# Linear attention and two MLPs on one core: the first eight steps of h written out in a set order

## The chip, the cores and the metric

One core of a Trainium2 chip runs the whole program. Its engines are named as the profile names them: PE (TensorE, matmuls; PEld its weight loads), DVE (VectorE), ACT (ScalarE), POOL (GpSimd) and SP (SyncE, which here issues loads and stores). The time is device microseconds of one execution, the median over several runs. Lower is better.

## The reference

```python
kv  = einsum('bhsd,bhse->bhde', k, v)          # batch 8, heads 8, seq 576, head_dim 64
out = einsum('bhsd,bhde->bhse', q, kv)
x   = out / sqrt(mean(out * out, -1) + 1e-6) * g_norm     # -> 4608 tokens x 512
h   = x @ w_in                                 # 512 -> 2048
x   = (h * cos(h)) @ w_out                     # 2048 -> 512
x   = ((x @ w1) * (x @ w2) @ w3) @ w_out2      # 512 -> 1024 -> 1024 -> 512
```

All values are float32.

## The kernel before

A token block is 512 tokens (nine blocks), a unit is half a batch, 288 tokens (16 units). Heads go in four pairs of 128 rows. The first MLP runs in steps n: in each, `emit_h` makes 128 columns of h (m) for a block (12 matmuls of 512 columns, since a float32 factor is split into a high and a low half and three products are summed), `g_first` and `g_rest` make g = h cos h of it on ACT and DVE, split into halves, and `emit_w(n-2)` adds g of two steps back to x (12 matmuls into four PSUM banks `acc0` to `acc3`). The order of the steps is m = 0 to 7 of block 0, then all 16 of block 1, then m = 8 to 15 of block 0, then the rest. Here x in the profile is the result of `emit_w`, and the operand of h too, by its tile.

The parts of g in a step: r = rounding of h / 2 pi (ACT), u = h / 2 pi - r (DVE), Sin (ACT), u times h (DVE), high half (ACT), low half (DVE).

The weights come in 32 blocks of 64-bit words in an order set by `first_pairs` (`i` for w_in, `u` for w_out: i0, i1, i2, u0, i3, u1, i4, u2, ...). `Chunk.convert` turns one block into float32: an absolute value on ACT (L141), then four passes on DVE (L142, L143, L146, L149). `put` splits the result into halves (ACT L112, DVE L114). The float rows of a block, u and others share five `row` buffers. Loads are issued by `prefetch`.

`load_first` issues the loads of the first two batches (k and v per pair `kvraw`, the last 64 rows of all pairs `kvrest` in one tile with one buffer, q per pair) between those of the first weight blocks, all on SP but two q loads. `first_batch` makes units 0 and 1: kv, out by a 128 x 128 matrix (`whole`, two heads on its diagonal), squares, sums of squares per token by matmuls, norms by a Newton iteration on DVE (`norms`), then `emit_rows`: the norms spread over partitions by 12 small matmuls for each unit and pair (`spread`), and one DVE product (L507). `split_x` makes the halves of x, the operand of h.

`second_batch` does the same for units 2 and 3 during steps 0 to 5 of the main loop. Its pieces are hung into steps by a plan with five places in a step: kv of pair p and unit 2 in step p, unit 3 one step later, the norms in step 5, and all rows of the spread behind them. Each out goes to one of two PSUM banks of `ps_a`, through the pool. All conversions of blocks from step 6 on are issued behind the norms (`second_last`). Block 1's x needs these units, so step 8 of h does too.

What sets the order: inside `tc.manual_schedule` PE, ACT and DVE take their instructions in the order of the program; before, that covers `first_batch` alone. All other work, SP's loads at all times too, is put in order by the scheduler of the framework, by readiness in its own model of time and by the order of the program; `tc.issue_after` adds an edge. On the chip each engine and SP's queue then take their instructions in that fixed order.

Of the kernel before, what the change touches and what calls it, by code (L numbers as in the profile page):

```python
# [1 line left out]

# [31 lines left out]
def kernel(  # L34
# [59 lines left out]
    def stage(shape, dtype, name):  # L94
        return ap.tile(shape, dtype, tag="stage", bufs=2, name=name)
# [311 lines left out]
    def load_first():  # L407

        def kv(b, p, q):
            t = wpool.tile(  # L410
                [P, 2, NC, P], F32, tag=f"wi{NM - 2 * NPAIR + p}", name=f"kvraw_{b}_{p}"
            )
            q.dma_start(
                out=t.rearrange("p i c f -> p (i c f)"),
                in_=kv_main[b, p].rearrange("p i c f -> p (i c f)"),
            )
            kv_raw[b, p] = t

        def rest(b, q):
            t = ap.tile([P, NPAIR // 2, 2, P], F32, tag="rest", name=f"kvrest_{b}")  # L420
            q.dma_start(
                out=t.rearrange("p g i f -> p (g i f)"),
                in_=kv_tail[b].rearrange("p g i f -> p (g i f)"),
            )
            kv_rest[b] = t

        def qs(b, p, q):
            t = wpool.tile([P, 2, HALF], F32, tag=f"wi{NM - NPAIR + p}", name=f"q_{b}_{p}")
            q_raw[b, p] = t
            q.dma_start(out=t, in_=qt[b, p].rearrange("u d s -> d u s"))  # L430

        qs(0, 0, nc.scalar)
        qs(0, 1, nc.scalar)
        for h in range(2):
            nc.scalar.dma_start(
                out=gneg[D * h:D * h + D], in_=g_norm.rearrange("(d o) -> d o", o=1)
            )
        kv(0, 0, nc.sync)
        rest(0, nc.sync)
        kv(0, 1, nc.sync)  # L440
        prefetch(1)
        kv(0, 2, nc.sync)
        qs(0, 2, nc.sync)
        prefetch(2)
        kv(0, 3, nc.sync)
        qs(0, 3, nc.sync)
        prefetch(7)
        for p in range(NPAIR):
            if p == NPAIR - 1:
                rest(1, nc.sync)  # L450
                prefetch(8)
            kv(1, p, nc.sync)
            qs(1, p, nc.sync)

    whole = []
# [4 lines left out]
            d = slice(D * h, D * (h + 1))  # L460
            nc.scalar.activation(whole[p][d, d], ps[d], AF.Copy)

    def emit_whole(u, p, pl, tag):
        ps = pl.tile([P, 512], F32, tag=tag, name=f"out_{u}_{p}")[:, 0:HALF]
        q = q_raw[u // NHALF, p][:, u % NHALF]
        nc.tensor.matmul(ps, whole[p], q, start=True, stop=True)
        o_ps[u, p] = ps

    squares = {}
    second_last = []  # L470

    def column(u, k, p):
        return ((u % NHALF * NT3 + k) * NPAIR + p) * 2
# [20 lines left out]
        nc.vector.tensor_scalar(x, sums[0:T3, 0:NR], EPS, HUGE, ALU.add, ALU.min)  # L494
        return newton(x, y, t)

    def emit_rows(u, p, ps, y, spread):
        for k in range(NT3):
            at = column(u, k, p)
            for h in range(2):  # L500
                mm = nc.tensor.matmul(
                    ps[D * h:D * h + D, T3 * k:T3 * k + T3],
                    y[:, at + h:at + h + 1].to_broadcast([T3, D]), spread,
                    start=k == 0, stop=True, skip_group_check=True,
                )
        o = o_sb[u][:, p, :]
        nc.vector.tensor_tensor(o, o, ps[:, 0:HALF], ALU.mult)  # L507
        return mm.ins

    def first_batch(spread, x, y, t):  # L510
# [19 lines left out]
        made = None  # L530
        for p in range(NPAIR):
            for u in units:
                emit_whole(u, p, ps_acc, f"acc{(2 * p + u) % 4}")
            for u in units:
                emit_square(u, p)
            if p == 0:
                made = pieces(count[0])
            rest_of(made)
            if p > 0:
                put(count[p - 1])  # L540
            if p + 1 < NPAIR:
                emit_kv(0, p + 1)
                copy_kv(p + 1)
            if p == 0:
                nc.vector.tensor_scalar(gneg, gneg, -1.0, None, ALU.mult)
            for u in units:
                emit_sums(u, p, sums, fresh=True)
            for u in units:
                emit_keep(u, p)
            if p + 1 < NPAIR:  # L550
                made = pieces(count[p + 1])
        norms(sums, x, y, t)
        put(count[-1])
        for p in range(NPAIR + 1):
            if p < NPAIR:
                for u in units:
                    ps = ps_acc.tile(
                        [P, 512], F32, tag=f"acc{(2 * p + u) % 4}", name=f"spread_{u}_{p}"
                    )
                    mm = emit_rows(u, p, ps, y, spread)  # L560
            if p > 0:
                last = split_x(0, p - 1)
        return mm, last

    def second_batch(spread, x, y, t):

        units = range(NHALF, 2 * NHALF)
        banks = {}

        def kv(p):  # L570
            if p == 0:
                banks[0] = ps_a.tile([P, 512], F32, tag="pa", name="kv_second")
            emit_kv(1, p, banks[0])

        def evac(u, p):
            emit_square(u, p)
            emit_keep(u, p)

        def sums(u, p):
            emit_sums(u, p, banks[0][:, NPAIR * D:NPAIR * D + NR])  # L580

        def rows(u, p):
            ps = ps_a.tile([P, 512], F32, tag="pa", name=f"spread_{u}_{p}")
            emit_rows(u, p, ps, y, spread)

        def last_norms():
            second_last.append(norms(banks.pop(0)[:, NPAIR * D:NPAIR * D + NR], x, y, t))

        plan = {}

        def at(n, i, f, *a):
            plan.setdefault(n, ([], [], [], [], []))[i].append(lambda: f(*a))

        a, b = units
        for p in range(NPAIR):
            at(p + 1, 0, emit_whole, b, p, ps_a, "pa")
            at(p + 1, 1, evac, b, p)
            at(p + 1, 3, sums, b, p)
        for p in range(NPAIR):
            at(p, 0, kv, p)  # L600
            at(p, 1, copy_kv, p)
            at(p, 2, emit_whole, a, p, ps_a, "pa")
            at(p, 2, evac, a, p)
            at(p, 3, sums, a, p)
        at(NPAIR + 1, 4, last_norms)
        for p in range(NPAIR):
            at(NPAIR + 1, 2 + p // 2, rows, a, p)
            at(NPAIR + 1, 2 + p // 2, rows, b, p)
        return plan

    NEWTON, LAST = 8, 10

# [44 lines left out]
    x0_d = dram.tile([P, KD, TB], F32, name="x0")  # L657
    part0_d = dram.tile([P, KD, TB], F32, name="part0")
    halfway = {}

    def save_x0():
        for u in range(2):
# [62 lines left out]
    def emit_w(n):  # L725
        t, m, first, last = steps[n]
        g = g_hl.pop(n)
        for j in range(KD):
            if first:
                acc[j] = ps_acc.tile([P, 512], F32, tag=f"acc{j}", name=f"x2_{n}_{j}")  # L730
            w = w_out[m][:, :, j * P:(j + 1) * P]
            three(acc[j], (w[:, 0], w[:, 1]), (g[:, 0], g[:, 1]), first, last)
        if last:
            for j in range(KD):
                s = row(f"x2s_{n}_{j}")
# [5 lines left out]
                    nc.vector.tensor_copy(s, acc[j])  # L741
                dst = part0_d[:, j] if m < NM - 1 else x2_d[:, j, t * TB:(t + 1) * TB]
                nc.sync.dma_start(out=dst, in_=s)

# [278 lines left out]
    if True:  # L1025
# [25 lines left out]
        with tc.manual_schedule(  # L1051
            engines={
                mybir.EngineType.DVE, mybir.EngineType.Activation, mybir.EngineType.PE
            }
        ):
            tiles = [spread] + [firsts[0:T3, T3 + NR * i:T3 + NR * i + NR] for i in range(3)]
            spread_last, split_last = first_batch(*tiles)
        behind = ExitStack()
        behind.enter_context(tc.issue_after(spread_last))
        for ins in split_last:  # L1060
            behind.enter_context(tc.issue_after(ins))
        second = second_batch(*tiles)

        NS = NB * NM
        ready = 4
# [6 lines left out]
            for u, s in zip(new, starts):  # L1072
                windows[u] = t * NM + s

        save_x0()
        since = []
        for n in range(NS + 2):
            t, m, first, last = steps[n] if n < NS else (NB, n - NS, False, False)
            swap = first and 0 < n
            if swap:  # L1080
                emit_w(n - 2)
            stages = []
            if n == NM + HM:
                load["alone"] = False
            ahead = 2 * n + 6 if n < 7 else 18 + (n - 7) * 6 // 5
            more = min(n_first, ahead) - state["conv"] if n < NS else 0
            if n < NS:
                with tc.issue_after(word_loads[min(n + 9, n_first - 6, len(word_loads) - 1)].ins):
                    stages = [
                        unit_stage(u, n - w) for u, w in windows.items() if 0 <= n - w <= LAST  # L1090
                    ]
                if n in second:
                    stages += [second[n]]
                    for f in second[n][4]:
                        f()
                if more > 0:
                    prefetch(min(state["conv"] + 8, n_first))
                    with tc.issue_after(second_last[0]) if second_last else nullcontext():
                        convert(more)
                emit_h(n)  # L1100
                uu = g_first(n)
            gate = ExitStack()
# [24 lines left out]
            with ExitStack() as gate:  # L1127
# [1 line left out]
                    for ins in since[:24][-3:] if n > 8 else ():  # L1129
                        gate.enter_context(tc.issue_after(ins))  # L1130
                run(stages, 3)
            if n == 7:
                behind.close()
            if n == NM + 4:
                load_halves("x0", x0_d)
            if n == 2 * NM - 4:
# [191 lines left out]
```

## Time and profile before

| | before |
|---|---|
| median of 3 runs | 1528.65 us (1527.91 to 1529.38) |
| profiled execution, own time | 1531.0 us |
| span of its trace | 1528.9 us |
| PE busy | 1491.9 us, 98% |
| DVE, ACT, POOL busy | 865.7, 674.6, 350.0 us |
| mean granted clock of PE | 0.985 |

The span runs from the first instruction to the last. Busy PE says that a matmul was in flight, not that PE ran at its peak; the granted clock is 1.00 at 2.4 GHz and 0.50 at 1.2 GHz. Of the page's 40 slices (38.2 us each) PE is below nine tenths in the first (six tenths) and the third (seven tenths), and the granted clock falls to seven tenths in the same two.

### The profile page before, as it was taken

The page shows a single profiled execution, that of the slowest core. Times are in us where ns is not written, and L with a number is a line of the kernel's source. Part 1 is how long each engine was busy: PE and PEld are TensorE (multiplying, and loading weights), DVE is VectorE, ACT ScalarE, POOL GpSimd, SP SyncE. Part 2 cuts the span into 40 slices and gives each one's busy share as a digit, 9 for nine tenths or more (in the row PEclk, how much of TensorE's full clock was granted, in tenths as well). Part 3 has the DMA queues.
Part 4 walks back from the last instruction along what each step waited for, and adds up shares of the span by engine and source line. Part 5 has one row for each costly group of instructions (what it writes and reads, how often), then busy time and mean ns, then how long its engine had stood idle before and what let it go on. Part 6 is the DMA issues. An engine that isn't in the chain of part 4 may idle for free.

```text
span 1528.9 us, 20580 instructions
## 1 busy us (share of the span) xinstructions
PE 1491.9 (98%) x7728; PEld 1275.0 (83%) x7728; DVE 865.7 (57%) x1559; ACT 674.6 (44%) x1355; POOL 350.0 (23%) x278
## 2 busy tenths in 40 slices
PE   6979999999999999999999998999999999999998
PEld 5757878878887887888888886999999988999997
DVE  5867845466565555555555337755545546545543
ACT  4635554544454454454535335443433334333331
POOL 0000010110010111101102006455444237344330
PEclk7979999999999999999999999999999999999999
DMA  9414330533423435334223015121112313233312
GB/s 361 155 43 147 102 91 17 157 106 106 126 86 109 140 105 150 89 109 130 89 73 101 10 41 193 42 76 67 67 40 83 110 57 104 82 104 125 124 62 76
DMA packets 81299, 155.02 MB, mean 101 GB/s; under 512 B 11232, under 2 KB 36944, under 8 KB 81200
## 3 DMA queue, kind: packets, MB, share of 16 engines
q1 hardware_dynamic: 80224, 152.08, 30.8%
q8 instruction: 60, 0.98, 0.3%
q0 software_dynamic: 272, 1.05, 0.2%
q10 hardware_dynamic: 704, 0.59, 0.1%
q14 instruction: 39, 0.32, 0.1%
HBM read 112.57 MB, written 41.12 MB: 101 GB/s over the span
## 4 chain that ended last, share of the span: by engine, by line
PE 93%; DVE 3%; DMA 1%; POOL 1%; issue 1%; SPq 0%; ACT 0%; DVEq 0%; ACTq 0%
PE X L928 13%; PE h L696 9%; PE x L696 9%; PE h L697 9%; PE h L698 9%; PE x L697 9%; PE x L698 9%; PE V L928 6%; PE o L697 4%; PE o L696 4%; PE o L698 4%; PE Y L928 3%; PE kv L277 1%; DMA i_w<-in_w1pair_dram 1%; DMA u_w<-in_w1pair_dram 1%
## 5 line engine op out<-in xcount | busy, mean ns | idle before, releaser
L928 PE MATMUL X<-xc,w 128*128 128x384 f32 x1152 | 226.3, 337 | 4.5 <-DVE wchl L114 2.3
L697 PE MATMUL x<-g,w_out 128*128 128x512 f32 x576 | 225.3, 391 | 0.0
L715 DVE SCALAR_TENSOR_TENSOR u<-h,r 128x512 f32<-128x512 f32 x144 | 99.5, 691 | 221.9 <-ACT r L713 218.3
L698 PE MATMUL x<-g,w_out 128*128 128x512 f32 x576 | 224.4, 390 | 0.0
L696 PE MATMUL x<-g,w_out 128*128 128x512 f32 x576 | 219.0, 392 | 0.0
L696 PE MATMUL h<-x,w_in 128*128 128x512 f32 x544 | 215.4, 396 | 3.0 <-DVE u L720 3.0
L928 PEld LDWEIGHTS X<-xc,w 128*128 128x128 f32 x1152 | 204.4, 189 | 12.0 <-ACT s L936 3.2
L697 PE MATMUL h<-x,w_in 128*128 128x512 f32 x544 | 214.1, 394 | 0.0
L698 PE MATMUL h<-x,w_in 128*128 128x512 f32 x544 | 213.2, 392 | 0.0
L114 POOL TENSOR_TENSOR xc<-x2r,xc 128x768 fp32r<-128x768 f32 x70 | 134.7, 1934 | 228.8 <-ACT xc L112 224.4
L713 ACT ACTIVATE r<-h 128x512 int32<-128x512 f32 x144 | 86.0, 597 | 220.6 <-PE h L698 210.8
L114 POOL TENSOR_TENSOR qhl<-q,qhl 128x288 fp32r<-128x288 f32 x48 | 41.1, 857 | 464.2 <-ACT qhl L112 464.2
L112 ACT ACTIVATE g<-u 128x512 fp32r<-128x512 f32 x144 | 90.9, 631 | 109.5 <-DVE u L720 83.0
L114 DVE TENSOR_TENSOR g<-u,g 128x512 fp32r<-128x512 f32 x144 | 104.4, 725 | 60.8 <-ACT g L112 60.7
L936 ACT ACTIVATE s<-X 128x384 f32<-128x384 f32 x144 | 66.6, 488 | 152.4 <-PE X L928 152.3
L696 PEld LDWEIGHTS x<-g,w_out 128*128 128x128 f32 x576 | 108.1, 188 | 22.9
L720 DVE TENSOR_TENSOR u<-u,h 128x512 f32<-128x512 f32 x144 | 98.6, 685 | 50.5 <-ACT u L719 50.3
L696 PEld LDWEIGHTS h<-x,w_in 128*128 128x128 f32 x544 | 103.0, 189 | 28.8 <-DVE u L720 7.0
L698 PEld LDWEIGHTS x<-g,w_out 128*128 128x128 f32 x576 | 108.2, 188 | 22.3
L697 PEld LDWEIGHTS x<-g,w_out 128*128 128x128 f32 x576 | 108.1, 188 | 22.2
L698 PEld LDWEIGHTS h<-x,w_in 128*128 128x128 f32 x544 | 102.8, 189 | 21.3
L697 PEld LDWEIGHTS h<-x,w_in 128*128 128x128 f32 x544 | 102.8, 189 | 20.2
(177 smaller groups left out, 2471.6 us busy)
## 6 DMA issues: line engine op xcount, KB each, us to landing
x2r<-x_all SPq DMA_DIRECT2D x44, 384.0 KB
kvraw<-in_kv_main_dram SPq DMA_DIRECT2D x32, 512.0 KB
x_all<-x2s SPq DMA_DIRECT2D x36, 256.0 KB
part<-o SPq DMA_DIRECT2D x36, 256.0 KB
part<-part SPq DMA_DIRECT2D x36, 256.0 KB
out_dram<-part SPq DMA_DIRECT2D x36, 256.0 KB
i_w<-in_w1pair_dram SPq DMA_DIRECT2D x16, 512.0 KB
u_w<-in_w1pair_dram SPq DMA_DIRECT2D x16, 512.0 KB
```

What stands on the lines that cost most here:

```text
L112: hi = nc.scalar.activation(dst[:, 0], src, AF.Copy)
L114: lo = lo_engine.tensor_tensor(dst[:, 1], src, f32(dst[:, 0]), ALU.subtract)
L277: nc.tensor.matmul(ps[d], k[:, d], v[:, d], start=fresh and i == 0, stop=i == NC, skip_group_check=True,)
L696: nc.tensor.matmul(ps, w[0], x[0], start=first, stop=False)
L697: nc.tensor.matmul(ps, w[0], x[1], start=False, stop=False)
L698: return nc.tensor.matmul(ps, w[1], x[0], start=False, stop=last).ins
L713: nc.scalar.activation(r, h_ps[n], AF.Identity, bias=0.25, scale=INV_2PI)
L715: nc.vector.scalar_tensor_tensor(u, h_ps[n], INV_2PI, r, ALU.mult, ALU.subtract)
L720: nc.vector.tensor_tensor(u, u, h_ps.pop(n), ALU.mult)
L928: nc.tensor.matmul(ps, w[:, self.i, a, k], x[:, b, k], start=first and k == 0 and n == 0, stop=last and k == 1 and n == 2, skip_group_chec ...
L936: copied.append(nc.scalar.activation(s, ps, AF.Copy).ins)
```

## The change

Steps 0 to 7 leave the main loop. A new function `first_steps` writes them out under `manual_schedule`, so PE, ACT and DVE take them in the order of the program. kv of pairs 0 and 1 of batch 1 is made in `first_batch`, ahead of the first norms; kv of pairs 2 and 3 in step 1. From step 2 on units 2 and 3 of one pair go together: each unit has one PSUM bank for its out of all pairs, and the sums of squares lie in the bank of unit 2. Two weight blocks are taken up in each of steps 0 to 5 (and two at the start), and converted in the next step, their DVE passes standing between the parts of g. The norms stand at the end of step 5, the spreads in steps 6 and 7, the split of x for block 1 in step 7. The rounding r goes to a `stage` buffer. The loads are put in another order in the program, and gneg's sign is turned on ACT. The main loop starts at step 8 with one block a step.

```diff
 load_first:
         qs(0, 3, nc.sync)
-        prefetch(7)
+        prefetch(6)
+        rest(1, nc.sync)
+        kv(1, 0, nc.sync)
+        kv(1, 1, nc.sync)
+        prefetch(8)
         for p in range(NPAIR):
-            if p == NPAIR - 1:
-                rest(1, nc.sync)
-                prefetch(8)
-            kv(1, p, nc.sync)
+            if p >= 2:
+                kv(1, p, nc.sync)
             qs(1, p, nc.sync)
 first_batch:
-                nc.vector.tensor_scalar(gneg, gneg, -1.0, None, ALU.mult)
+                nc.scalar.activation(gneg, gneg, AF.Copy, scale=-1.0)
...
+        for p in range(2):
+            emit_kv(1, p)
         norms(sums, x, y, t)
         put(count[-1])
+        for p in range(2):
+            copy_kv(p)
-    def second_batch(spread, x, y, t):
...
+    def first_steps(spread, x, y, t):
...
+        def begin():
+            st = chunks[state["conv"]].convert()
+            state["conv"] += 1
+            next(st)
+            return st
+        def each():
+            for st in pair:
+                next(st)
+        def out_bank(v, p):
+            if p == 0:
+                banks[v] = ps_a.tile([P, 512], F32, tag="pa", name=f"out_{v}")
+            emit_whole(v, p, banks[v][:, 0:HALF])
+        def rows(p):
+            for v in units:
+                spread_ps[v, p] = ps_a.tile([P, 512], F32, tag="pa", name=f"spread_{v}_{p}")
+                emit_rows(v, p, spread_ps[v, p], y, spread, False)
+        def scale(p):
+            for v in units:
+                o = o_sb[v][:, p, :]
+                ps = spread_ps.pop((v, p))
+                nc.vector.tensor_tensor(o, o, ps[:, 0:HALF], ALU.mult)
+        prefetch(min(state["put"] + 8, n_first))
+        pair = [begin(), begin()]
+        for n in range(HM):
+            p = n - 2
+            last = n == HM - 1
+            emit_h(n)
+            if n == 1:
+                for k in (2, 3):
+                    emit_kv(1, k)
+                    copy_kv(k)
+                for v in units:
+                    out_bank(v, 0)
+            if 0 <= p < NPAIR:
+                for v in units:
+                    emit_square(v, p)
+                sums = banks[units[0]][:, HALF:HALF + NR]
+                for v in units:
+                    emit_sums(v, p, sums)
+            if n == NPAIR + 2:
+                rows(0)
+            if n >= 2:
+                emit_w(n - 2)
+            if n == 0:
+                for _ in range(3):
+                    each()
+            if last:
+                scale(1)
+                rows(2)
+            r = stage([P, TB], I32, f"r_{n}")
+            u = row(f"u_{n}")
+            nc.scalar.activation(r, h_ps[n], AF.Identity, bias=0.25, scale=INV_2PI)
+            nc.vector.scalar_tensor_tensor(u, h_ps[n], INV_2PI, r, ALU.mult, ALU.subtract)
+            if n > 0:
+                each()
+                each()
+            nc.scalar.activation(u, u, AF.Sin, bias=HALF_PI, scale=TWO_PI)
+            if last:
+                for c in range(2):
+                    split_x(1, c)
+            new = [begin()] if n < HM - 2 else []
+            nc.vector.tensor_tensor(u, u, h_ps.pop(n), ALU.mult)
+            if n > 0:
+                each()
+            if last:
+                scale(2)
+                rows(3)
+            g_hl[n] = m1.tile([P, 2, TB], F32R, tag="g", bufs=2, name=f"g_{n}")
+            since.extend([h_last.pop(n), *split(g_hl[n], u, nc.vector)])
+            new += [begin()] if n < HM - 2 else []
+            if 0 <= p < NPAIR:
+                for v in units:
+                    emit_keep(v, p)
+            if 1 < n <= NPAIR:
+                for v in units:
+                    out_bank(v, n - 1)
+            if n == NPAIR + 2:
+                scale(0)
+                rows(1)
+            each()
+            put(len(pair))
+            pair = new
+            prefetch(min(state["put"] + 8, n_first))
+            if n == NPAIR + 1:
+                norms(sums, x, y, t)
+        split_x(1, 2)
+        scale(3)
+        made = split_x(1, 3)
+        return [emit_w(HM - 2), *made]
 the main loop:
-        for n in range(NS + 2):
+        for n in range(HM, NS + 2):
...
-            ahead = 2 * n + 6 if n < 7 else 18 + (n - 7) * 6 // 5
+            ahead = 12 + n
...
-                    with tc.issue_after(second_last[0]) if second_last else nullcontext():
-                        convert(more)
+                    convert(more)
```

Here NPAIR is 4 and HM is 8.

## Rows read from the trace of the kernel before

**Rows 1.** The page, chain of waits by engine.

```profile
PE 93%; DVE 3%; DMA 1%; POOL 1%; issue 1%; SPq 0%; ACT 0%; DVEq 0%; ACTq 0%
```

**Rows 2.** Windows: stretch, length, busy per engine (instructions), granted clock, DMA, GB/s.

```profile
41.00:91.80 50.80, 50.24 (x302) 40.26 (x300) 32.13 (x63) 30.38 (x67) 0.26 (x1) 1.00 0.31 104
...
114.00:116.80 2.80, 2.80 (x8) 2.22 (x7) 1.81 (x3) 0.63 (x1) 0.00 (x0) 0.50 0.00 0
116.80:120.00 3.20, 3.20 (x15) 2.65 (x15) 0.00 (x0) 0.00 (x0) 0.00 (x0) 1.00 0.00 0
```

**Rows 3.** Timeline of PE: start, us, instruction; in brackets the idle before it.

```profile
94.56 1.21 PE L501 MATMUL spread<-rs_first 96*64 96x96 f32 x24 [2.75 <-DVE rs_first L370]
96.85 2.26 PE L501 MATMUL spread<-rs_first 96*64 96x96 f32 x24 [1.07 <-DVE o L507]
...
111.22 0.79 PE L696 MATMUL h<-x,w_in 128*128 128x512 f32 x1 [2.83 <-DVE u L720]
...
116.87 0.39 PE L696 MATMUL h<-x,w_in 128*128 128x512 f32 x1
```

**Rows 4.** Timeline of DVE: the first operation of the norms, the first behind them.

```profile
91.86 0.20 DVE L494 TENSOR_SCALAR rs_first<-kv_second 96x48 f32<-96x48 f32 x1 [2.02 <-PE kv_second L488]
...
94.34 0.42 DVE L142 TENSOR_SCALAR i_f<-i_f 128x512 f32<-128x512 f32 x1
```

**Rows 5.** Groups of PE, 38 to 112 us: busy us, mean ns.

```profile
L698 PE MATMUL x<-g,w_out 128*128 128x512 f32 x24 | 9.5, 394 | 0.0
```

**Rows 6.** Timeline of PE in the first batch.

```profile
19.46 0.48 PE L277 MATMUL kv<-kvrest 64*64 64x64 f32 x4
...
31.82 7.29 PE L501 MATMUL spread<-rs_first 96*64 96x96 f32 x96 [5.38 <-DVE rs_first L370]
```

**Rows 7.** Timeline of SP's queue: when each load is issued.

```profile
10.85 0.44 SPq L132 DMA_DIRECT2D u_w<-in_w1pair_dram  x1
...
19.50 0.33 SPq L132 DMA_DIRECT2D i_w<-in_w1pair_dram  x1
...
24.36 0.33 SPq L132 DMA_DIRECT2D u_w<-in_w1pair_dram  x1
...
27.70 0.33 SPq L421 DMA_DIRECT2D kvrest<-in_kv_tail_dram  x1
...
33.73 0.33 SPq L132 DMA_DIRECT2D u_w<-in_w1pair_dram  x1
```

**Rows 8.** The chain in order of time: start, us, what.

```profile
10.85 8.57 DMA u_w<-in_w1pair_dram
```

**Rows 9.** Timeline of DVE: last splits of the first batch, then neighbours of each kind.

```profile
39.65 1.42 DVE L114 TENSOR_TENSOR x<-o,x 128x288 fp32r<-128x288 f32 x4
...
97.05 0.41 DVE L143 TENSOR_SCALAR u_f<-u_f 128x512 int32<-128x512 int32 x1
97.39 0.44 DVE L507 TENSOR_TENSOR o<-o,spread 128x288 f32<-128x288 f32 x1
97.75 0.67 DVE L146 SCALAR_TENSOR_TENSOR i_f<-i_w,i_f 128x512 int32<-128x512 int32 x1
98.35 0.67 DVE L146 SCALAR_TENSOR_TENSOR u_f<-u_w,u_f 128x512 int32<-128x512 int32 x1
```

**Rows 10.** Timeline of ACT: two copies of kv; square, keep, block, Sin in a row.

```profile
44.20 0.43 ACT L461 ACTIVATE rs_first<-kv_second 64x64 f32<-64x64 f32 x2
...
70.02 0.41 ACT L479 ACTIVATE sq<-out 128x288 f32<-128x288 f32 x1 [1.75 <-PE out L466]
70.32 0.50 ACT L482 ACTIVATE o<-out,gneg 128x288 f32<-128x288 f32 x1
70.70 0.67 ACT L141 ACTIVATE i_f<-i_w 128x512 f32<-128x512 f32 x1
71.28 0.61 ACT L719 ACTIVATE u<-u 128x512 f32<-128x512 f32 x1
```

**Rows 11.** Timeline of PE: out of one unit and pair.

```profile
74.70 0.73 PE L466 MATMUL out<-q,rs_first 128*128 128x288 f32 x2
```

More of the change, by code (lines that the diff above doesn't have):

```diff
@@ L1 @@
-from contextlib import ExitStack, nullcontext
+from contextlib import ExitStack
 import concourse.bass as bass
@@ L461, in copy_kv, with emit_whole @@
             nc.scalar.activation(whole[p][d, d], ps[d], AF.Copy)
-    def emit_whole(u, p, pl, tag):
-        ps = pl.tile([P, 512], F32, tag=tag, name=f"out_{u}_{p}")[:, 0:HALF]
+    def emit_whole(u, p, ps):
         q = q_raw[u // NHALF, p][:, u % NHALF]
@@ L469 @@
     squares = {}
-    second_last = []
     def column(u, k, p):
@@ L495, in norms, with emit_rows @@
         return newton(x, y, t)
-    def emit_rows(u, p, ps, y, spread):
+    def emit_rows(u, p, ps, y, spread, scaled=True):
         for k in range(NT3):
@@ L505, in emit_rows @@
                 )
-        o = o_sb[u][:, p, :]
-        nc.vector.tensor_tensor(o, o, ps[:, 0:HALF], ALU.mult)
+        if scaled:
+            o = o_sb[u][:, p, :]
+            nc.vector.tensor_tensor(o, o, ps[:, 0:HALF], ALU.mult)
         return mm.ins
@@ L532, in first_batch @@
             for u in units:
-                emit_whole(u, p, ps_acc, f"acc{(2 * p + u) % 4}")
+                emit_whole(u, p, ps_acc.tile(
+                    [P, 512], F32, tag=f"acc{(2 * p + u) % 4}", name=f"out_{u}_{p}"
+                )[:, 0:HALF])
             for u in units:
@@ L561, in first_batch @@
             if p > 0:
-                last = split_x(0, p - 1)
-        return mm, last
-    def second_batch(spread, x, y, t):
+                split_x(0, p - 1)
+    def first_steps(spread, x, y, t):
         units = range(NHALF, 2 * NHALF)
-        banks = {}
-        def kv(p):
-            if p == 0:
[L572 to L609, printed above, removed]
@@ new lines, in first_steps @@
+        banks, spread_ps = {}, {}
+        def begin():
[7 more added lines that the diff above has]
+        def out_bank(v, p):
+            if p == 0:
+                banks[v] = ps_a.tile([P, 512], F32, tag="pa", name=f"out_{v}")
[4 more added lines that the diff above has]
+                emit_rows(v, p, spread_ps[v, p], y, spread, False)
@@ new lines, in scale @@
+        def scale(p):
+            for v in units:
+                o = o_sb[v][:, p, :]
+                ps = spread_ps.pop((v, p))
+                nc.vector.tensor_tensor(o, o, ps[:, 0:HALF], ALU.mult)
+        prefetch(min(state["put"] + 8, n_first))
[62 more added lines that the diff above has]
+                norms(sums, x, y, t)
@@ L659 @@
     halfway = {}
+    since = []
     def save_x0():
@@ L731, in emit_w @@
             w = w_out[m][:, :, j * P:(j + 1) * P]
-            three(acc[j], (w[:, 0], w[:, 1]), (g[:, 0], g[:, 1]), first, last)
+            mm = three(acc[j], (w[:, 0], w[:, 1]), (g[:, 0], g[:, 1]), first, last)
         if last:
@@ L743, in emit_w @@
                 nc.sync.dma_start(out=dst, in_=s)
+        return mm
     PAIR = {1: (0, 0), 2: (1, 1), 3: (6, 2), 4: (2, 6), 5: (3, 3), 6: (4, 4), 7: (5, 5)}
@@ L1056 @@
             tiles = [spread] + [firsts[0:T3, T3 + NR * i:T3 + NR * i + NR] for i in range(3)]
[L1057 to L1062, printed above, removed]
+            first_batch(*tiles)
+            save_x0()
+            behind = first_steps(*tiles)
         NS = NB * NM
@@ L1073 @@
                 windows[u] = t * NM + s
-        save_x0()
-        since = []
-        for n in range(NS + 2):
+        gates = ExitStack()
+        for ins in behind:
+            gates.enter_context(tc.issue_after(ins))
+        for n in range(HM, NS + 2):
             t, m, first, last = steps[n] if n < NS else (NB, n - NS, False, False)
             swap = first and 0 < n
-            if swap:
+            if swap and n > HM:
                 emit_w(n - 2)
@@ L1091 @@
                     ]
[L1092 to L1095, printed above, removed]
                 if more > 0:
                     prefetch(min(state["conv"] + 8, n_first))
-                    with tc.issue_after(second_last[0]) if second_last else nullcontext():
-                        convert(more)
+                    convert(more)
                 emit_h(n)
@@ L1131 @@
                 run(stages, 3)
-            if n == 7:
-                behind.close()
+            if n == HM + 1:
+                gates.close()
             if n == NM + 4:
```

## The prediction

> **What bounds the kernel now.** I read the chain of waits first. 93% of it is TensorE (PE) [rows 1], so a change pays only where PE stands idle or runs at the lower of its two clock levels (1.2 GHz, shown as 0.50; the higher, 2.4 GHz, as 1.00). The windows come second: from 41.0 to 91.8 us PE is dense at 1.00, then comes a hole, and from 116.8 on it is dense at 1.00 again; a step of h and a step of x, 12 matmuls each, flow at 3.20 us / 14 = 0.23 us a matmul there, 2.76 us a step [rows 2]. The hole lies around the norms of units 2 and 3: PE waits 2.75 us for the last Newton operation of VectorE (DVE), the clock falls, and step 8 of h starts at 111.22 after another wait of 2.83 us and stays at 0.50 until 116.8 [rows 2, 3]. The norms take from 91.86 to 94.34, 2.48 us [rows 4]. In the hole PE does nothing but 96 tiny spread matmuls. Step 8 of h stands behind steps 0 to 7, and 72 matmuls of x are issued by then (three lines of 24, so steps 0 to 5) [rows 5]; at 116.87 step 8 and one matmul of step 9 are through as well. From there nothing in front of PE is late. So I work out when the changed kernel reaches the same amount of PE work; that difference is the answer.
>
> **The change, part by part.** Sums are made against the profiled execution: span 1528.9, own time 1531.0, which is 2.35 above the median 1528.65. A difference in the span is put on both.
>
> *The first batch.* kv of pairs 0 and 1 of batch 1 moves ahead of the first norms, into a stretch where PE waits: after the sums it idles until the spread starts at 31.82 [rows 6]. 40 small matmuls by themselves cost nothing there. But PE takes its instructions in order, and each kv ends with four matmuls on the rest tile (kvrest). That tile has one buffer, so its second load can't be issued before kv(0,3) has read the first, which ends at 19.46+0.48=19.9 [rows 6]. In what order SP issues is set by the scheduler, for SP isn't among the three engines in set order: i5 of a much later step left at 19.50, ahead of rest(1), which left at 27.70 although rest(1) stands earlier in the program [rows 7]. SP also runs eight loads ahead and no more: u_w, issued at 10.85, landed 8.57 later at 19.42 [rows 8], and the eighth issue behind it left at 19.50; so u3, issued 24.36, landed at 33.73, when the eighth behind it left [rows 7]. Between u_w and u3 lie nine loads of 512 KB and two of 288 KB (q), 5184 KB in 33.73-19.42=14.3 us: 1.4 us for 512 KB, 0.8 for a q, 0.7 for the rest tile's 256 KB. Behind u3 come q(1,2), kv(1,3) and rest(1), so rest(1) lands at 33.73+0.8+1.4+0.7=36.6 in its present place, at 35.2 if it goes ahead of kv(1,3). In the new program text it stands further up, but its readiness, kv(0,3), is the same; I take 35.2. Then PE still has the rest of kv(1,0), 0.4, and kv(1,1), about 1.5 at the lower clock (20 matmuls, of which the last four take 0.48 [rows 6], the other 16 about 1.0): the spread starts at 37.1 instead of 31.8, **5.3 us late**. All of this was under no cover but the wait for the norms, which ends at 31.8. The ends: 0 (the load lands before 29.9) and 6.7. The negation of gneg moves from DVE to ScalarE (ACT) and shortens ACT's wait for it, but the first batch then waits for u_w at 19.42 [rows 8] as before: 0.
>
> *Step 0.* After the last split of the first batch DVE is free at 39.65+1.42=41.07 [rows 9] (all times now without the 5.3). It first runs three passes over two blocks, 2x0.34+2x0.34+2x0.6=2.54, so its first operation on h stands at 43.6. The spacings are 0.34 for a TENSOR_SCALAR, 0.60 for the others of 512 columns, 0.36 for a scale, and a 512-column result is there 0.67 after its start [rows 9]. Step 0 has no passes between its parts of g: 0.67, Sin 0.6, 0.67, hi 0.62, lo 0.6, two passes 1.2, then the puts; before r of step 1 ACT still has both hi halves and the four copies of kv(1,2) and kv(1,3), two of which took 0.43 [rows 10]. That is 6.7 us.
>
> *Steps 1 to 5.* DVE has per step 3x0.6 for g, 3.76 for two blocks, 1.2 for their lo halves: 6.8. Were that all, a step would last 7.45 (behind the last hi half, at 6.3, come two squares of 0.3 and r, 0.6 [rows 10]); so step 1. In steps 2 to 4 a loop through three engines is longer. From the start of DVE's first operation: u and four passes 1.96, product ready 2.63, hi 3.27, one block's Abs 0.58 to 3.85, two keeps 0.38 each and their end, 4.7 [rows 9, 10]. Only then may the out bank be overwritten: the out of two units, two matmuls each that last 0.73 with their end [rows 11], so about 1.3 together, and behind these in PE's order the next h: 2.76, its result 0.3 later (a matmul lasts 0.39, and the next one starts after 0.23 [rows 2, 5]), r 0.6: **9.65 us a step**, of which PE idles about 2. Three such steps are 29. Step 5 has no out bank but the norms at its end: 6.95+2.48=9.4 [rows 4].
>
> *Steps 6, 7.* PE has run out of work when h of step 6 is through, some 3.9 us before the norms end. In the kernel before, a wait of 2.75 and one of 1.07 a little later made the clock fall: the same 24 spread matmuls took 1.21 ahead of the second wait and 2.26 behind it [rows 3], so I take the lower clock here, until 5.6 us after PE resumes (111.22 to 116.8). The spread of pair 0 (24 matmuls) 2.3, x of step 4 until 6.7, the spread of pair 1 1.2, h of step 7 2.76 + 0.3, r 0.6: 11.6. At full clock it would be 9.9. In step 7 u, Sin, two column blocks of the x split, the product, two scales and the spread of pair 3 stand in one line until 5.75; x of step 6 and h of step 8 follow at 2.76 each: 11.3.
>
> *The sum.* 43.6+6.7+7.45+29+9.4+11.6+11.3=119.05 for the end of step 8 of h, with x of step 6 done. Before, PE stood 11 matmuls further back at 116.87: 116.87+11x0.23=119.4. So the set order by itself gains 0.35. Against it stand 5.3 for the rest tile, and 0.9 for the clock in step 2: PE waits from 46.5 to 49.8 for the copies of kv and from 53.3 to 57.3 for the squares of pair 0, both longer than the 2.75 of [rows 3], so the sums and x of step 0 start at the lower clock (13 matmuls in 116.87-111.22: 0.43 each), which lasts 5.6 us as there, and end at 63.4, 0.9 behind the keeps at 62.5. 0.35-5.3-0.9 = -5.85. For steps 3 and 4 I take no fall of the clock, bounds 0 and 4.8 (2.4 more for each h at 0.43). Behind step 8 both kernels are dense: 0. Against the profiled execution 1531.0+5.85=1536.85; against the median **1534.5 us**.
>
> One rule of the Trainium skill weighs against the change: "TensorE: Matmul & The Clock Gate", section on PSUM-queue depth-cycling, tells of a kernel in which short idle times between matmul groups, as PSUM banks go round, make the clock swing. This trace shows a fall after waits of 2.75 and 1.07 us [rows 3], and no wait of 2 us between dense groups. By the rule the later steps would swing too and the sum be that of the first rival, 1538.1; by the row, as I read it, 1534.5.
>
> **Rivals.**
> *The clock falls in every step.* For it: the same waits come back each 9.65 us. Against it: a step at the lower clock leaves PE no idle time, so it climbs again. Three h steps at 0.43 cost 3x2.4=7.2, half of that if every other one climbs: 1534.5+3.6=1538.1, at most 1541.7.
> *The rest tile is in time* (not slower). Place: SP's queue. If the scheduler puts rest(1) so far up that SP stands still for it from 13.5 until 19.9, it lands some 4 us later, and kv is hidden. Decides: a landing before 29.9 costs nothing and leaves -0.55, and at 32.4 the loss passes 0.2%. For it: the program text has rest(1) ahead of kv(1,0). Against it: [rows 7]. 1534.5-5.3=1529.2; if the clock also holds in step 6 (1.7), 1527.5, faster by a little.
> *The loop through keep, out and h doesn't bind*, as where out is issued ahead of its place or ACT gets to the keeps sooner: 3x(9.65-7.45)=6.6 less: 1527.9, and 1522.6 with the rest tile in time, which is faster. Against it: three engines in set order.
>
> **How the numbers follow.** The forecast holds 0.40 (its own range 1531.5 to 1537.5), the clock 0.14, the rest tile in time 0.23, the loop 0.17, anything else 0.06. 0.2% is 3.06 us, about what a measurement can tell: under 1525.6 faster, over 1531.7 slower. Slower: 0.35 of the forecast, 0.13 of the clock, 0.03 of the rest tile, 0.01 of the loop = 0.52. Faster: 0.07 of the rest tile, 0.10 of the loop where both go well, 0.03 of the others = 0.20. Same: 0.28. The range 1524.5 to 1540 takes in both early cases and the clock's up to near its end.
>
> **What would show it.** Right: PE's wait ahead of kv's rest matmuls is put down to the DMA of kvrest, with the spread starting at 36 to 38 us; steps 2 to 4 are 9.65 us apart on DVE's first operation, with an idle PE of about 2 us ahead of out, released by ACT; the hole of 91.8 to 116.8 is gone, in its place a wait of about 4 us for the norms some 20 us sooner in PE's work. Wrong: a spread that starts at 32, steps of 7.5 us, or a clock of 0.50 over most of 60 to 90 us.

## The result and the profile after

The changed kernel takes 1538.92 us (median of 6 runs, 1533.6 to 1540.61) against 1528.26 us (6 runs, 1527.75 to 1529.38): ratio 1.0065, 95% interval 1.0049 to 1.0080. It is 10.7 us slower; 5.85 were forecast, and 1538.92 lies above the forecast's own range (1531.5 to 1537.5), inside the whole range (1524.5 to 1540). Its runs lie 7 us apart, those of before 1.6. The profiled executions differ by less (own times 1537.59 and 1531.0, spans 1535.5 and 1528.9), since that of before stands 2.7 above its median and that of after 1.3 below.

In the first batch, on PE's timeline (start, us, instruction, idle before it), the spread that answers to the one at 31.82 [rows 6] stands at 38.03:

```profile
26.38 1.12 PE L277 MATMUL kv<-kvraw 128*64 128x64 f32 x16
36.17 0.48 PE L277 MATMUL kv<-kvrest 64*64 64x64 f32 x4 [8.66 <-DMA kvrest<-in_kv_tail_dram]
...
37.62 0.48 PE L277 MATMUL kv<-kvrest 64*64 64x64 f32 x4
38.03 6.11 PE L501 MATMUL spread<-rs_first 96*64 96x96 f32 x96
```

and SP's queue shows its load in the very place that it had [rows 7], though it stands further up in the program:

```profile
26.63 0.33 SPq L413 DMA_DIRECT2D kvraw<-in_kv_main_dram  x1
27.93 0.33 SPq L421 DMA_DIRECT2D kvrest<-in_kv_tail_dram  x1
```

DVE's first operation on h of each step shows the steps' lengths (a wait in brackets):

```profile
49.34 0.68 DVE L633 SCALAR_TENSOR_TENSOR u<-h,r 128x512 f32<-128x512 f32 x1
...
56.12 0.69 DVE L633 SCALAR_TENSOR_TENSOR u<-h,r 128x512 f32<-128x512 f32 x1 [0.74 <-ACT r L632]
...
63.54 0.69 DVE L633 SCALAR_TENSOR_TENSOR u<-h,r 128x512 f32<-128x512 f32 x1 [0.39 <-ACT r L632]
...
73.17 0.69 DVE L633 SCALAR_TENSOR_TENSOR u<-h,r 128x512 f32<-128x512 f32 x1 [2.34 <-ACT r L632]
...
82.64 0.69 DVE L633 SCALAR_TENSOR_TENSOR u<-h,r 128x512 f32<-128x512 f32 x1 [2.34 <-ACT r L632]
...
92.09 0.69 DVE L633 SCALAR_TENSOR_TENSOR u<-h,r 128x512 f32<-128x512 f32 x1 [2.31 <-ACT r L632]
...
101.63 0.68 DVE L633 SCALAR_TENSOR_TENSOR u<-h,r 128x512 f32<-128x512 f32 x1
...
116.67 0.69 DVE L633 SCALAR_TENSOR_TENSOR u<-h,r 128x512 f32<-128x512 f32 x1 [2.88 <-ACT r L632]
```

That is 6.8, 7.4, 9.6, 9.5, 9.45, 9.5 and 15.0 us for steps 0 to 6. ACT's timeline shows the high half of g in steps 3 and 6, and what it waits for:

```profile
76.35 0.63 ACT L112 ACTIVATE g<-u 128x512 fp32r<-128x512 f32 x1 [1.25 <-PE x L759]
...
108.39 0.63 ACT L112 ACTIVATE g<-u 128x512 fp32r<-128x512 f32 x1 [5.42 <-PE x L759]
```

And PE in steps 3 and 6, where the spreads answer to those of [rows 3]:

```profile
77.97 1.24 PE L467 MATMUL out<-q,rs_first 128*128 128x288 f32 x4 [1.66 <-ACT o L482]
...
101.85 2.19 PE L501 MATMUL spread<-rs_first 96*64 96x96 f32 x24 [3.90 <-DVE rs_first L370]
103.97 0.80 PE L757 MATMUL x<-g,w_out 128*128 128x512 f32 x1
...
110.26 2.15 PE L501 MATMUL spread<-rs_first 96*64 96x96 f32 x24 [1.90 <-DVE o L600]
112.34 0.80 PE L757 MATMUL h<-x,w_in 128*128 128x512 f32 x1
```

The windows (columns as in [rows 2]) give the clock: 1.00 behind the wait of 1.66 us of step 2, 0.50 behind the wait of 3.90 us for the norms, and 0.52 once more behind the wait of 1.90 (from 78 to 97 us, behind the waits of 1.66 of steps 3 and 4, it is 1.00 too):

```profile
68.50:76.20 7.70, 7.70 (x40) 6.20 (x40) 5.26 (x11) 3.97 (x8) 0.00 (x0) 1.00 0.39 136
97.80:101.80 4.00, 0.16 (x1) 0.00 (x0) 3.56 (x15) 1.19 (x3) 0.00 (x0) 0.79 0.00 0
101.80:106.70 4.90, 4.85 (x31) 4.08 (x31) 3.65 (x8) 0.63 (x1) 0.00 (x0) 0.50 0.00 0
106.70:108.30 1.60, 1.60 (x7) 1.05 (x5) 0.00 (x0) 0.00 (x0) 0.00 (x0) 0.93 0.00 0
110.20:113.70 3.50, 3.44 (x27) 3.05 (x28) 3.40 (x7) 1.23 (x2) 0.00 (x0) 0.52 0.27 50
```

Step 8 of h and one matmul of step 9 are through at 127.93, with x of step 6 done. Before, the same without x of step 6 stood at 116.87 [rows 3], so at 119.6 with its twelve matmuls: 8.3 us later. The first matmul of the second MLP (X) stands 6.5 later (956.4 and 949.9). Of the 1.8 between, 0.9 are shorter waits of PE for ACT ahead of wc, the product of w3 and w_out2 (2.0 us in all, 2.9 before); where the rest comes back was not followed.

### The profile page after: what moved, and what is told of

Its sections match the earlier page's. It is cut to its first block, busy times and chain, and to the rows that moved or that the text cites. A ratio compares the mean times of both kernels' runs of the same rounds, so it can differ in the third digit from the quotient of the medians.

```text
span 1535.5 us, 20577 instructions
## 1 busy us (share of the span) xinstructions
PE 1490.5 (97%) x7728; PEld 1273.7 (83%) x7728; DVE 866.8 (56%) x1558; ACT 675.0 (44%) x1356; POOL 349.3 (23%) x278
## 4 chain that ended last, share of the span: by engine, by line
PE 91%; DMA 3%; DVE 2%; ACT 1%; POOL 1%; issue 1%; SPq 0%; ACTq 0%; DVEq 0%
PE X L990 13%; PE x L757 9%; PE x L758 9%; PE h L757 9%; PE x L759 8%; PE h L758 8%; PE h L759 8%; PE V L990 6%; PE o L758 4%; PE o L757 4%; PE o L759 4%; PE Y L990 3%; PE kv L277 2%; DMA q<-in_qt_dram 1%; DMA u_w<-in_w1pair_dram 1%
## 5 line engine op out<-in xcount | busy, mean ns | idle before, releaser
L776 DVE SCALAR_TENSOR_TENSOR u<-h,r 128x512 f32<-128x512 f32 x136 | 93.9, 691 | 216.7 <-ACT r L774 212.0
L774 ACT ACTIVATE r<-h 128x512 int32<-128x512 f32 x136 | 81.1, 597 | 212.7 <-PE h L759 203.2
L114 DVE TENSOR_TENSOR g<-u,g 128x512 fp32r<-128x512 f32 x144 | 102.9, 714 | 63.1 <-ACT g L112 62.9
L781 DVE TENSOR_TENSOR u<-u,h 128x512 f32<-128x512 f32 x136 | 93.0, 684 | 47.4 <-ACT u L780 47.3
```

The costliest lines, as they stand in the source:

```text
L114: lo = lo_engine.tensor_tensor(dst[:, 1], src, f32(dst[:, 0]), ALU.subtract)
L774: nc.scalar.activation(r, h_ps[n], AF.Identity, bias=0.25, scale=INV_2PI)
L776: nc.vector.scalar_tensor_tensor(u, h_ps[n], INV_2PI, r, ALU.mult, ALU.subtract)
L781: nc.vector.tensor_tensor(u, u, h_ps.pop(n), ALU.mult)
```

## The experiments

Each was timed beside the kernel before, whose medians there were 1529.67 and 1529.53. Since the chip's own level moves by a us, differences from the changed kernel are taken between ratios: 1.0065 less the kernel's own, times 1529. The intervals of the ratios reach 0.0009 to 0.0016 to either side, so such a difference is known to about 3 us either way (an estimate from these intervals); what a step gained is read from the traces.

**The rest tile in a buffer of its own.**

```diff
-            t = ap.tile([P, NPAIR // 2, 2, P], F32, tag="rest", name=f"kvrest_{b}")
+            pl, tag = (wpool, "wo7") if b else (ap, "rest")
+            t = pl.tile([P, NPAIR // 2, 2, P], F32, tag=tag, name=f"kvrest_{b}")
```

> The rest tile of batch 1 gets a buffer of its own (that of w_out 7, first needed in step 6), so its load needn't wait for kv(0,3). Theory A, the wait for the rest tile delays everything behind it: the load leaves behind u1 at about 13 us and lands near 24, PE no longer waits 8.66 us ahead of kv's rest matmuls, the spread starts at 32 instead of 38.0, and the first operation on h on DVE moves from 49.3 to about 43.6: 5.7 us less, 1533.2 against 1538.9. Theory B, the loads as a whole set the start of the steps: the 8.66 us turn into waits of ACT for the blocks of step 0 or of kv(1,1), and less than 1 us is gained.

1534.29 us, 1.0029 (1.0019 to 1.0040): 5.5 us less than the changed kernel. PE's wait for the tile is gone and the spread starts before 32; its own DVE shows 6.15 us at step 0, of which step 2 gives 1.55 back (11.2 us instead of 9.6):

```profile
43.19 0.68 DVE L634 SCALAR_TENSOR_TENSOR u<-h,r 128x512 f32<-128x512 f32 x1
...
57.39 0.69 DVE L634 SCALAR_TENSOR_TENSOR u<-h,r 128x512 f32<-128x512 f32 x1 [0.39 <-ACT r L633]
...
68.57 0.69 DVE L634 SCALAR_TENSOR_TENSOR u<-h,r 128x512 f32<-128x512 f32 x1 [2.33 <-ACT r L633]
```

Its windows say why: x of step 0 runs at 0.50 there, the clock fall that was forecast for step 2 and that the changed kernel's profiled execution did not have at this place (1.00 from 62.7 to 66.7).

```profile
58.70:61.00 2.30, 2.30 (x7) 1.82 (x6) 2.30 (x6) 0.64 (x2) 0.00 (x0) 0.50 0.33 132
```

Theory A holds, B falls.

**kv of pairs 0 and 1 back into step 0.**

```diff
-        for p in range(2):
-            emit_kv(1, p)
         norms(sums, x, y, t)
         put(count[-1])
-        for p in range(2):
-            copy_kv(p)
...
             if n == 0:
+                for k in (0, 1):
+                    emit_kv(1, k)
                 for _ in range(3):
                     each()
...
             new = [begin()] if n < HM - 2 else []
+            if n == 0:
+                for k in (0, 1):
+                    copy_kv(k)
```

> kv of pairs 0 and 1 goes back out of the first batch, into step 0 behind h of step 0 on PE; its copies stand behind Sin on ACT. The rest tile keeps its single buffer. Theory A: the spread starts at 31.8, 5.7 us less, and the 1.8 us of kv matmuls fall into PE's wait of step 1 for the copies (2.95 us): 1533.2, as with the tile of its own. Theory B: kv's place makes no difference, or kv pushes h of step 1 and its step back by its 1.8 us: 1537 or more.

1535.40 us, 1.0035 (1.0023 to 1.0047): 4.6 us less. The spread starts at 31.89. Step 0 lasts 7.6 us instead of 6.8 (42.96 to 50.52), so the place of kv cost 0.8 in step 0, not nothing. Step 2 lasts 11.15 us here, as with the buffer of its own. Two ways of taking the same wait away agree within their intervals.

**x of step 4 ahead of the spread in step 6.**

```diff
-            if n == NPAIR + 2:
-                rows(0)
             if n >= 2:
                 emit_w(n - 2)
+            if n == NPAIR + 2:
+                rows(0)
```

> In step 6 x of step 4 goes ahead of the spread of pair 0 on PE; nothing else is moved. Theory C, in step 6 the high half of g waits for x of step 4 because g has two buffers, and x stands behind a spread that waits for the norms, at the lower clock: the wait of ACT for x (5.42 us) goes, step 6 from DVE's first operation to the next falls from 15.0 to about 10, and PE's wait ahead of the spread falls from 3.9 to about 1.2, so that its clock holds: 5 us less, 1533.9. Theory D, only the clock's fall is to blame: 1.7 us less, 1537.2. Theory E, the norms set the end of step 6 whatever PE does: no change.

1536.71 us, 1.0043 (1.0031 to 1.0056): 3.4 us less, where theory C said 5 and D 1.7. Step 6 fell from 15.0 to 11.2, not to 10. PE's timeline shows the rest: the first spread now runs at full clock (1.21), but the second waits longer, for the scale of pair 0 on DVE, and falls to half (2.02):

```profile
101.11 1.21 PE L501 MATMUL spread<-rs_first 96*64 96x96 f32 x24 [1.18 <-DVE rs_first L370]
...
105.72 2.02 PE L501 MATMUL spread<-rs_first 96*64 96x96 f32 x24 [3.41 <-DVE o L600]
```

The time alone, 3.4 us, does not part C from D. The trace does: the high half of g no longer waits for x (it starts at 103.59, behind DVE's product), so C is right in kind, and the scale's place in DVE's order is late next.

**The keeps ahead of the high half of g.**

```diff
             new = [begin()] if n < HM - 2 else []
+            if 0 <= p < NPAIR:
+                for v in units:
+                    emit_keep(v, p)
+            if 1 < n <= NPAIR:
+                for v in units:
+                    out_bank(v, n - 1)
             nc.vector.tensor_tensor(u, u, h_ps.pop(n), ALU.mult)
```

(and the same lines taken out behind the split of g)

> In steps 2 to 5 the two keeps move ahead of the high half of g on ACT, so the out bank is free while x of two steps back still runs on PE. Theory F, the steps of 9.5 us are a ring: x of two steps back frees g's buffer, then hi 0.6, a block 0.55, keeps 0.87, out 0.86, h 2.8, sums 0.96, x 2.8; with the keeps out of the ring PE's wait of 1.66 to 2 us ahead of out goes and steps 2 to 4 fall to about 7.7 us: 5 us less, 1533.7. Theory G, the two blocks per step on DVE set the step: 9.5 stays, no change.

1533.68 us, 1.0027 (1.0018 to 1.0036): 5.8 us less. Steps 3 and 4 last 7.67 and 7.65, against 9.5, and PE has no wait ahead of out any more; step 2, at 9.3, had the lower clock (0.64 from 63.1 to 66.0):

```profile
73.16 0.69 DVE L633 SCALAR_TENSOR_TENSOR u<-h,r 128x512 f32<-128x512 f32 x1 [0.41 <-ACT r L632]
...
80.83 0.69 DVE L633 SCALAR_TENSOR_TENSOR u<-h,r 128x512 f32<-128x512 f32 x1 [0.41 <-ACT r L632]
...
88.48 0.69 DVE L633 SCALAR_TENSOR_TENSOR u<-h,r 128x512 f32<-128x512 f32 x1 [0.42 <-ACT r L632]
```

Theory F holds and G falls. The 7.65 that remain are not DVE's blocks either: from one first operation to the next PE is busy all 7.67 us at full clock, DVE 7.02:

```profile
73.16:80.83 7.67, 7.67 (x42) 6.21 (x42) 7.02 (x13) 5.52 (x11) 0.00 (x0) 1.00 0.41 131
```

**A third buffer for g.**

```diff
-            g_hl[n] = m1.tile([P, 2, TB], F32R, tag="g", bufs=2, name=f"g_{n}")
+            if n in (2, 5):
+                g_hl[n] = wpool.tile([P, 2, TB], F32R, tag=f"wi{12 + n // 3}", name=f"g_{n}")
+            else:
+                g_hl[n] = m1.tile([P, 2, TB], F32R, tag="g", bufs=2, name=f"g_{n}")
```

> g of steps 2 and 5 gets buffers of its own (those of w_in 12 and 13, not yet needed), so the high half of g no longer waits for x of two steps back in steps 2, 4, 5 and 6; all orders stay. If g's two buffers close the ring of 9.5 us, the wait of ACT for x (five times, 12 us together) goes; in steps 2 to 4 hi moves up from 3.2 to 2.65 behind DVE's first operation, but the keeps still stand behind hi and out behind the keeps, so these steps fall by 0.5 each; step 6 falls from 15.0 to about 13, since PE's order and the low clock stay: 3.5 us less, 1535.4. Rival: the ring is closed by the keeps alone, less than 1 us.

1532.77 us, 1.0025 (1.0016 to 1.0034): 6.1 us less. In its trace steps 2 to 4 last 8.99, 8.96 and 8.97 (0.5 to 0.6 less each; 0.5 was said) and step 6 12.2 (2.9 less): 4.5 together. What the timed runs have beyond that was not found, and is within the intervals. ACT's waits for x are gone. Both the keeps and g's buffers stand in the ring; without the buffers' wait the chain through the product stays, at 9.0.

**Three edits together, and h of step 7 ahead of the second spread.** The three edits are those above. A further kernel adds a fourth:

```diff
-            emit_h(n)
+            if n < HM - 1:
+                emit_h(n)
...
                 scale(0)
+                emit_h(n + 1)
                 rows(1)
```

With the three edits:

> Three edits together: the rest tile's own buffer, x of step 4 ahead of the spread in step 6, and the keeps ahead of hi. Alone they gave 5.5, 3.4 and 5.8 us. If they stand for three separate stretches of one chain they add up, less 1 to 2 us for the clock in step 2, which falls behind a PE wait of 3 us as it did with the rest tile alone: 13 us less than the changed kernel, 1526, which is 2 us under the kernel before. Rival: they share a loss (the clock, or DVE behind them all), and together give 8 us or less: 1531.

1524.59 us, 0.9967 (0.9957 to 0.9977): 15 us less than the changed kernel, and 0.3% faster than the kernel before. Alone the three gave 5.5, 3.4 and 5.8, 14.7 in sum: within the intervals they add up, as three stretches of one chain would.

With the fourth too:

> The three edits, and h of step 7 on PE ahead of the spread of pair 1, in the 3.4 us in which PE waited for the scale of pair 0. If step 6 is then held by DVE alone it lasts about 8.5 instead of 11.2, and PE doesn't fall to the lower clock there: 2.5 us less than without it, 1524. Rival: the scales of pairs 1 to 3 in step 7 hold the end anyway: no further gain.

1522.88 us, 0.9956 (0.9944 to 0.9969). Step 6 falls to 8.4 us (91.98 to 100.38) from 12.2 with the three edits, as the first theory says. In the time the gain over the three edits is 1.7 us; the two intervals overlap, so it is not shown. Of the 3.8 us of step 6, 1.6 are lost again in this trace to the clock in step 2 (9.3 us for 7.7).

**The kernel before, with the blocks not held behind the norms.**

```diff
-                    with tc.issue_after(second_last[0]) if second_last else nullcontext():
+                    with nullcontext():
                         convert(more)
```

> The kernel before, with one edit: the conversion of blocks in steps 6 to 9 no longer stands behind the norms of units 2 and 3. DVE sat idle for 12 of the 15 us from 79 to 94, then had four blocks to convert and put (10 us) in the hole among the scales and splits that PE waited for. Theory H, these blocks make the hole long: it shrinks from 20 us (91.2 to 111.2) to 12 or less and the time falls by 6 to 10 us, to 1519 to 1523. Rival: the hole is norms, spread and clock by themselves, less than 2 us is gained, and the change's aim of filling it by a set order was the only way.

1517.04 us, 0.9919 (0.9905 to 0.9932): 12.5 us less than before, more than was said, and faster than both kernels and every other version here. The rival falls. The hole is not so much shortened as filled. On PE's timeline the norms have matmuls of x around them, the spreads stand between those of h, and the clock stays at 1.00 until 104 (before, behind the norms, the spreads ran at the lower clock: [rows 3]):

```profile
96.31 0.39 PE L698 MATMUL x<-g,w_out 128*128 128x512 f32 x1
96.67 2.48 PE L501 MATMUL spread<-rs_first 96*64 96x96 f32 x48
99.08 0.73 PE L696 MATMUL h<-x,w_in 128*128 128x512 f32 x2
99.74 0.71 PE L501 MATMUL spread<-rs_first 96*64 96x96 f32 x12
...
110.89 0.50 PE L696 MATMUL h<-x,w_in 128*128 128x512 f32 x1 [2.99 <-DVE u L720]
```

The windows of the same kernel, columns as in [rows 2]:

```profile
91.00:94.00 3.00, 3.00 (x15) 2.50 (x15) 2.84 (x8) 0.63 (x1) 0.00 (x0) 1.00 0.01 3
94.00:98.00 4.00, 3.94 (x38) 2.97 (x39) 2.93 (x12) 0.72 (x2) 0.00 (x0) 1.00 0.02 4
98.00:104.00 6.00, 6.00 (x66) 4.29 (x68) 4.15 (x11) 2.26 (x6) 0.00 (x0) 1.00 0.00 0
111.70:114.70 3.00, 3.00 (x9) 2.32 (x8) 3.00 (x6) 1.93 (x4) 0.00 (x0) 0.50 0.44 170
```

DVE's timeline tells why. In the kernel before it idles for 9.20 us, and its first operations on h of steps 6 and 7 come last:

```profile
89.18 0.66 DVE L114 TENSOR_TENSOR x<-o,x 128x64 fp32r<-128x64 f32 x4 [9.20 <-ACT x L112]
...
107.64 0.67 DVE L715 SCALAR_TENSOR_TENSOR u<-h,r 128x512 f32<-128x512 f32 x1
...
108.61 0.67 DVE L715 SCALAR_TENSOR_TENSOR u<-h,r 128x512 f32<-128x512 f32 x1
```

Without the edge these two stand at:

```profile
82.69 0.69 DVE L715 SCALAR_TENSOR_TENSOR u<-h,r 128x512 f32<-128x512 f32 x1
...
89.24 0.68 DVE L715 SCALAR_TENSOR_TENSOR u<-h,r 128x512 f32<-128x512 f32 x1
```

g of steps 6 and 7 had stood behind the held blocks on DVE, so x of these steps was not to be had during the norms: 96 matmuls of x are issued by 96.6 us without the edge, 72 before. That one edge kept DVE idle for 9.2 us up to 89 and then made it late. One wait of 2.99 us is left, and behind it the clock falls to 0.50 (last window).

## Why the prediction was right, and where its sizes were off

*The first batch.* Right as a mechanism, place and releaser; 5.3 us were taken and 6.2 measured on PE (38.03 for 31.82); DVE's first operation on h stands at 49.34, 5.7 behind the forecast's 43.6. The load kept its place behind kv(1,3), for which the forecast had 6.7 as its upper end, and PE's 96 spread matmuls took 6.1 instead of 7.3. Both ways of undoing it gave 4.6 to 5.5 us in the time.

*Steps 0 to 5.* 6.7, 7.45, 9.65 three times and 9.4 were forecast; 6.8, 7.4, 9.6, 9.5, 9.45 and 9.5 measured. The way to 9.65 was partly wrong. I had hi start with the product, at 2.63; it starts at 3.2, since g has two buffers and the third waits for x of two steps back (the 1.25 above). Two outs take 0.86 until h starts, not 1.3. That the two errors cancelled was luck; the keeps and the third buffer show the real ring. (The three passes in front of step 0 add up to 2.56, not 2.54, and the 6.95 of step 5 stands without a working; neither moves the sum.) The rival that this loop doesn't bind fell: moved out of it, the keeps gave 5.8 us.

*Step 6.* The step that failed: "The spread of pair 0 (24 matmuls) 2.3, x of step 4 until 6.7, the spread of pair 1 1.2, h of step 7 2.76 + 0.3, r 0.6: 11.6". It lasted 15.0. What goes ahead of it was right: PE's wait for the norms (3.9 forecast, 3.90 measured) and the fall of the clock behind it. But I had the scale of pair 0 run beside x on DVE, and hi of step 6 waits for the buffer that x of step 4 holds (5.42 us), so the split, the scale and the second spread stand behind x, and the clock falls a second time. Putting x first took 3.8 us off the step and 3.4 off the time, a third buffer 2.9 off the step.

*Steps 7 and 8, the sum.* 11.3 were forecast, and 11.26 measured (116.67 to 127.93). By the forecast's own sum step 8 ends at 125.25, so it came 2.7 late: 3.4 from step 6, 0.4 from the first batch, less about 1.2 in steps 0 to 5, most of it the 0.9 for the clock in step 2, which this execution did not pay.

*The clock.* Two waits of 3.3 and 4.0 us were forecast in steps 1 and 2, and a fall behind the second, in x of step 0 (0.9). In the changed kernel's trace the waits are 2.95 and 2.13, and the fall comes behind the first, in h of step 2 (0.50 from 57 to 59 us). There it costs nothing: PE would only have waited longer for the squares (3.73 us in the trace with the keeps moved, where h of step 2 ran at full clock), and the sums start 7.72 us behind the out in both. In four of the seven experiments on the changed kernel x of step 0 did run at the lower clock, for 1.5 to 1.6 us of step 2, so the term is real, but not in every trace. The rival of a fall in every step fell: three waits of 1.66 us left the clock at 1.00, and 1538.92 stands at this rival's number, 1538.1, by chance. By the rule of the Trainium skill in "TensorE: Matmul & The Clock Gate", section on PSUM-queue depth-cycling, as the prediction used it, these steps would have swung; this trace does not agree. Which waits do make the clock fall, these traces do not settle (last section).

*The rest tile in time* fell in the changed kernel, and came true in the experiment that gives it a buffer: 5.5 us there, 5.3 in the forecast.

*The rest.* Between the two profiled executions the change costs 6.6 us, close to the 5.85. Part of this is luck: step 8 is 8.3 us late, and 1.8 come back behind it, where the forecast had 0. The medians of the timed runs differ by 4 us more, which is the 2.7 and the 1.3 by which the two profiled executions miss their medians. Why single runs of the changed kernel lie up to 7 us apart stays open. The mean clocks recorded with them do not put them in order (0.986 at 1537.59 and at 1540.61 us, 0.993 at 1540.00, 0.989 at 1533.6).

## What to carry to other kernels

An instruction put early into the order of an engine that takes its work in turn brings all its operands' waits with it: look up the last one to land (here a 256 KB tile with one buffer) before its own cost. When the steps of a pipeline are written out by hand, follow each buffer around the ring once, the double-buffered ones first. And before a stall is filled by a new order, look for an edge that holds back the work that would fill it: one line did more here (12.5 us) than the new order with its three faults mended (4.9 us, 6.7 with the fourth edit).

## What the runs showed of the hardware that was not expected

TensorE's clock answered to one and the same wait in two ways. The changed kernel and the one with the keeps moved have the same program up to step 2. Ahead of the first out PE waits for ACT in both. In the changed kernel the clock falls behind this wait (PE's timeline, then a window with the columns of [rows 2]):

```profile
55.05 1.66 PE L467 MATMUL out<-q,rs_first 128*128 128x288 f32 x4 [2.95 <-ACT rs_first L463]
57.00:59.00 2.00, 2.00 (x6) 1.58 (x5) 2.00 (x6) 1.27 (x3) 0.00 (x0) 0.50 0.37 135
```

With the keeps moved it does not, and falls behind the next wait:

```profile
55.40 1.24 PE L467 MATMUL out<-q,rs_first 128*128 128x288 f32 x4 [2.97 <-ACT rs_first L463]
55.40:59.40 4.00, 4.00 (x16) 2.86 (x16) 3.26 (x8) 2.48 (x6) 0.00 (x0) 1.00 0.65 232
...
63.12 1.41 PE L488 MATMUL out<-sel,sq 128*96 128x2 f32 x12 [3.73 <-ACT sq L479]
63.10:67.00 3.90, 3.88 (x18) 3.39 (x19) 3.51 (x8) 2.74 (x6) 0.00 (x0) 0.60 0.69 249
```

Nor does the length of the last wait decide alone: with the rest tile in its own buffer x of step 0 fell to 0.50 though PE had waited only 0.93 us ahead of the sums (a wait of 2.84 us and a stretch at 0.50 had ended some 8 and 2 us sooner), and in the changed kernel it ran at 1.00 behind 2.13 us. Each kernel was traced once, so what decides is open.
